# A routed two-layer kernel: its last three 128-row blocks go behind a branch on a count made on the chip

## The chip, the cores and the metric

One core of a Trainium2 chip runs the whole program. The metric is the device time of one execution in microseconds (us). Engines are named as in the profile: PE (TensorE matmuls), PEld (its weight loads), DVE (VectorE), ACT (ScalarE), POOL (GpSimd) and SP (SyncE, which issues DMAs here). A "q" behind an engine's name (POOLq, SPq) is its sequencer.

## What is computed

The input is x (8 x 3584 x 192). A softmax-weighted causal convolution of 7 taps per head group makes 28672 tokens of 192 values. Each token goes to the one of 8 experts whose embedding is nearest by cosine, and leaves it scaled by the gate weight:

```python
x = attn_out.reshape(B * S, D)                  # 28672 x 192
logits = xn @ en.T / tau
expert_idx = np.argmax(logits, axis=1)
for e in range(E):                              # 8 experts
    mask = expert_idx == e
    h = np.maximum(x[mask] @ w1[e], 0.0)        # 192 -> 1024
    out[mask] = gate_w[mask, None] * (h @ w2[e])  # 1024 -> 192
```

How many tokens an expert gets is known only when the program runs.

## The kernel before

**Routing.** The tokens come in 16 chunks of 1792. For each chunk, `mix` convolves, `route` and `rank` find the expert of every token and its place in that expert's list, and `scatter` (L626) writes the token's row (values in fp16 pairs, token number, gate weight) to `rows_d` in DRAM. Each expert has its own area there; behind the eight areas lies a dummy area. `pads` (L637) writes, behind each expert's list and into the dummy area, pad rows whose token number is N = 28672.

**Blocks.** The expert phase works on blocks of 1024, 512, 256 or 128 rows of one expert. The program's list of blocks, `self.subs`, is fixed when it is built; what each block holds is found on the chip by `select` (L656): from the counts so far it makes, per block, the offset of its expert's weights and its first row. `pick` (L836) calls it: as many blocks of n rows as are certain to exist, whatever the split over experts. Only in the last round, for n = 128, are the blocks rounded up: with `left` = 1792 rows not yet handed out, `pick(128, True)` makes (1792 + 8 x 127) // 128 = 21 blocks, which is enough for any split. In that call `select` counts the blocks that hold rows, expert by expert; `a` (L671) is their running sum, so its last element is their number. The blocks behind that number get the dummy area's address (L692 to L696).

**The last round.** `last_blocks` (L918) hands out 3 blocks of 1024 rows (each two sub-blocks of 512), 8 of 512, 8 of 256 and the 21 of 128, after all routing. It sorts them by keys so that the sizes alternate: the i-th of n in a class has the key (i + o) / (n + o), with o = 0.5 for the large and the middle class and 3 for the 128-row class. Written with A for a (sub-)block of 512 rows, M for 256 and s for 128, the order is

```
before: A A s A A A s s A s A s A s s A s A A A s s M s M s s M s M s A A s M s M s s M s M s
```

**One block** is `expert` (L772). A 128-row block takes its weights by two DVE copies into a slot: `copy_w1` (L717, copy at L729), which the preceding block issues at its end (L808), and `copy_w2` (L731). Then PE makes 40 matmuls into `h_ps` (L796); ACT writes relu (L800) and DVE the low half of the pair (L802), each in two instructions of 512 columns; DVE makes the gate factors `g` (L811); PE makes 24 matmuls into `o_ps` (L819); ACT scales (L824); POOL scatters 128 rows to the output by an indirect DMA (L826). Its `bounds_check=self.N - 1` with `oob_is_err=False` leaves out rows whose token number is N. A block of 512 has 40 wide matmuls and 96 of `o_ps`, one of 256 has 40 and 48. `fetch` (L736) loads a block's rows by two transposing DMAs and its token numbers by a third, from SP, up to three blocks ahead; there are three buffers `e_xT`.

**Order.** SP's queue stands in the order of the Python code. PE, DVE, ACT and POOL get theirs from the framework's scheduler, which lets the next block's `h_ps` matmuls fill PE's time between two parts of a block's `o_ps` matmuls. `run` (L930) drives all: its main loop (L985) ends when routing is done and all blocks are issued.

Of the kernel before, what the change touches and what calls it, by code (L numbers as in the profile page):

```python
# [15 lines left out]
I32 = mybir.dt.int32  # L16
# [10 lines left out]
E = 8  # L27
# [33 lines left out]
LEAD = 16.0  # L61
CAP = 6.0
MARGIN = 22
AHEAD_STEPS = 36


# [8 lines left out]
class _Moe:  # L75
# [580 lines left out]
    def select(self, n, k, last, name, cb):  # L656
        nc, cp = self.nc, self.cp
# [12 lines left out]
        a, ap, bs = one("a"), one("ap"), one("bs")  # L670
# [9 lines left out]
            out=ge[:, :, 1:], in0=a[:].unsqueeze(1).to_broadcast([1, k, E]),  # L680
# [4 lines left out]
            out=df, in0=df, in1=bs[:].unsqueeze(1).to_broadcast([1, k, E]),  # L685
# [3 lines left out]
        nc.vector.scalar_tensor_tensor(out=ro, in0=jf, scalar=float(n), in1=ro,  # L689
                                       op0=ALU.mult, op1=ALU.add)  # L690
        if last:
            nc.vector.tensor_scalar(out=tm, in0=jf, scalar1=-float(n),  # L692
                                    scalar2=float(self.dummy), op0=ALU.mult,
                                    op1=ALU.add)
            nc.vector.tensor_tensor(out=tm, in0=tm, in1=ge[:, :, E], op=ALU.mult)
            nc.vector.tensor_tensor(out=ro, in0=ro, in1=tm, op=ALU.add)  # L696
# [6 lines left out]
        if not last:  # L703
# [6 lines left out]
                out=self.start, in0=t, scalar=float(n), in1=self.start,  # L710
# [184 lines left out]
    def steer(self, spent):  # L895
# [9 lines left out]
        self.rate = min(self.rate, 3.0)  # L905
        self.pace = (NT * self.end - self.nput) / max(1.0, steps - MARGIN)
        if self.final:
            self.pace = 1.0
        early = 0
        for v in self.subs[self.at:]:  # L910
            if len(v) == 5 and v[4] > len(self.scatters):
                self.pace = max(self.pace, (v[4] - len(self.scatters))
                                / max(1.0, early - AHEAD_STEPS))
                break
# [3 lines left out]
    def last_blocks(self):  # L918
        self.now, self.final = self.cb[0:1, :], True
        self.need = len(self.scatters) + len(self.pend) + E + 1  # L920
        big = self.pick(1024)
        mid = self.pick(512) + self.pick(256)
        self.pads()
        small = self.pick(128, True)
        runs = [[((i + o) / (len(g) + o), b) for i, b in enumerate(g)]
                for g, o in ((big, 0.5), (mid, 0.5), (small, 3.0)) if g]
        for _, b in sorted(sum(runs, []), key=lambda v: v[0]):
            self.subs += b

    def run(self):  # L930
        self.left, self.rate = 0, 1.0
# [21 lines left out]
        done = dict.fromkeys(work, 0)  # L953
# [19 lines left out]
        a = self.dispatch()  # L973
# [8 lines left out]
            if i.engine in (self.nc.vector.engine, self.nc.scalar.engine):  # L982
                _dep(self.tc, i, end[i.engine].name, False)
        live, due, done, out = next(a, None), [0.0, 0.0], False, 0.0
        while live or self.pend or not done or self.at < len(self.subs):  # L985
            if self.at < len(self.subs):
                for v in self.expert():
                    self.steer(spent)
                    self.clock += STEP[v is OUT]
                    out = min(1.0, out + self.pace)  # L990
                    if out >= 1.0 and self.pend:
                        self.put(self.step)
                        out -= 1.0
                    due = [min(CAP, d + self.rate * t) for d, t in zip(due, v)]
                    while live and min(due) >= 0.0:
                        held = live is WAIT
                        if not held:
                            due = [d - t for d, t in zip(due, live)]
                            spent = [s + t for s, t in zip(spent, live)]
                        live = next(a, None)  # L1000
                        if held and live is WAIT:
                            break
            else:
                self.put()
                self.clock += 1.0
                if live:
                    live = next(a, None)
            if not live and not done:
                self.last_blocks()
                done = True  # L1010
        order.__exit__(None, None, None)


@with_exitstack
# [17 lines left out]
```

## Time and profile before

| | |
|---|---|
| time, median of 3 runs | 1249.96 us (1249.76, 1249.96, 1250.8) |
| the profiled execution: its own time | 1245.91 us |
| its span, first to last instruction | 1244.2 us |
| mean granted TensorE clock | 0.961 |
| PE busy | 1135.9 us (91%) |
| DVE, ACT, POOL busy | 61%, 48%, 44% |
| output scatters (L826) | 231 |
| matmuls of `o_ps` (L819) | 5544 |

The profiled execution took 4.05 us less than the median of the three runs. Engine rows of a timeline give the start in us from the span's start, the duration, the engine, the line, the operation, output and inputs, and how many instructions are merged; in brackets stands the idle time of the engine just before, and what ended it. Successive rows of PE overlap a little, as matmuls are pipelined; the differences between their starts don't. The page names in its third section the DMA queues: q0 carries the indirect DMAs of POOL, q8 and q14 carry instructions.

### The profile page before, as it was taken

To read this page: it belongs to the slowest core of one execution; us is meant where nothing else is said; L and a number is where in the kernel's file an instruction comes from. 1 tells how busy PE (TensorE), PEld (TensorE's weight loads), DVE (VectorE), ACT (ScalarE), POOL (GpSimd) and SP (SyncE) were. 2 spreads that over 40 slices of the span, in tenths; PEclk is the share of its full clock that TensorE was granted. 3 is DMA by queue.
4 is the path that set the end of the run, shared out by engine and by line. 5 is a ranking of instruction groups with operands and counts; after the bars stand their busy time and mean duration, and the time that the engine had idled before them with its cause. 6 is when DMAs were issued, how large, how long until landed. Compare 5 with 4: busy or idle time off the path is not lost.

```text
span 1244.2 us, 31794 instructions
## 1 busy us (share of the span) xinstructions
PE 1135.9 (91%) x10620; PEld 881.2 (71%) x10620; DVE 763.8 (61%) x2042; ACT 592.5 (48%) x1359; POOL 552.6 (44%) x525
## 2 busy tenths in 40 slices
PE   4765869899999899998999999989999999999998
PEld 2543758776677876766887667757877786898797
DVE  3899667885766856666766474653335544465364
ACT  4986335455564464563546463333333434333333
POOL 0074166573565554646745456672222121222222
PEclk9676889999999999999999999999999999999999
DMA  9745576566666596654657645333222131223121
GB/s 255 216 146 147 120 162 147 119 168 145 135 157 165 97 185 146 131 140 97 165 105 170 115 94 125 87 96 66 65 45 61 41 75 43 43 54 72 42 52 28
DMA packets 305962, 140.69 MB, mean 113 GB/s; under 512 B 247774, under 2 KB 296285, under 8 KB 305808
## 3 DMA queue, kind: packets, MB, share of 16 engines
q1 hardware_dynamic: 282000, 87.97, 34.1%
q0 software_dynamic: 23808, 50.69, 14.7%
q8 instruction: 94, 1.54, 0.5%
q14 instruction: 60, 0.49, 0.1%
HBM read 38.35 MB, written 51.35 MB: 72 GB/s over the span
## 4 chain that ended last, share of the span: by engine, by line
issue 27%; PE 15%; POOL 8%; DMA 2%; ACT 1%; DVE 1%; POOLq 1%; ACTq 0%; DVEq 0%
POOL out_dram L826 7%; PE h_ps L796 7%; PE o_ps L819 6%; PE conv_ps L388 1%; DMA rows_d<-rows,di 1%; POOL rows_d L627 1%; DMA out_dram<-y,e_mt 1%; DMA xtb<-rows 0%; POOLq L826 0%; ACT work L800 0%; ACT sq L401 0%; PE lg_ps L611 0%; ACT rows L437 0%; DVE work L802 0%; DVE rows L444 0%
## 5 line engine op out<-in xcount | busy, mean ns | idle before, releaser
L819 PE MATMUL o_ps<-work 128*128 128x192 f16 x5544 | 503.2, 248 | 21.1 <-DVE work L802 9.2
L819 PEld LDWEIGHTS <-work 128*128 128x128 f16 x5544 | 462.5, 98 | 60.4 <-DVE work L802 15.7
L826 POOL DMA_INDIRECT out_dram<-y,e_mt x231 | 257.0, 1113 | 479.1 <-ACT y L824 439.2
L802 DVE SCALAR_TENSOR_TENSOR work<-h_ps,work 128x512 f16<-128x512 f32 x462 | 314.4, 685 | 175.2 <-ACT work L800 169.7
L800 ACT ACTIVATE work<-h_ps 128x512 f16<-128x512 f32 x462 | 271.3, 596 | 240.3 <-PE h_ps L796 206.1
L627 POOL DMA_INDIRECT rows_d<-rows,di x256 | 281.2, 1098 | 140.7 <-issue 57.1
L796 PE MATMUL h_ps<-e_xT,res 128*128 128x512 f16 x1360 | 311.2, 380 | 8.5 <-DVE work L802 5.9
L796 PEld LDWEIGHTS <-res 128*128 x1360 | 131.5, 98 | 162.7 <-issue 20.2
L796 PE MATMUL h_ps<-e_xT,work 128*128 128x256 f16 (+1 forms) x2320 | 232.4, 256 | 14.8 <-DMA e_xT<-rows_d 10.6
L796 PEld LDWEIGHTS <-work 128*128 128x128 f16 x2320 | 193.6, 99 | 40.7 <-DMA e_xT<-rows_d 9.9
L824 ACT ACTIVATE y<-o_ps,g 128x192 f32<-128x192 f32 x231 | 94.2, 419 | 235.6 <-PE o_ps L819 213.7
L732 DVE COPY work<-res 128x3074 f16 x88 | 85.3, 969 | 163.9 <-PE o_ps L819 163.8
L388 PE MATMUL conv_ps<-xt,band 128*112 128x384 f32 x256 | 112.5, 542 | 13.6 <-ACT xt L391 5.2
L437 ACT CAST rows<-xt 112x768 f16<-112x768 f32 x64 | 53.0, 832 | 97.4 <-DMA rows_d<-rows,di 49.2
L391 ACT COPY xt<-conv_ps 112x384 f32<-112x384 f32 x128 | 60.4, 480 | 43.0 <-PE conv_ps L388 41.5
L401 ACT ACTIVATE sq<-xt 112x192 bf16<-112x192 f32 x204 | 73.6, 361 | 4.8
L444 DVE TENSOR_TENSOR rows<-xt,rows 112x512 f16<-112x512 f32 x64 | 43.9, 685 | 45.7 <-ACT rows L437 35.3
L388 PEld LDWEIGHTS conv_ps<-xt,band 128*112 128x112 f32 x256 | 42.8, 194 | 32.0 <-issue 13.1
L435 DVE TENSOR_TENSOR xt<-xt,x_p_s 112x768 f32<-112x768 f32 x64 | 58.5, 950 | 0.0
L729 DVE COPY work<-res 128x3072 f16 x58 | 55.5, 957 | 0.3 <-PE h_ps L796 0.3
L611 PEld LDWEIGHTS <-xtb 128*128 128x128 f16 x768 | 30.1, 98 | 26.1 <-DMA xtb<-rows 12.9
L611 PE MATMUL lg_ps<-ma,xtb 128*128 128x16 f16 x512 | 30.6, 171 | 14.0 <-ACT xtb L502 7.1
(157 smaller groups left out, 520.5 us busy)
## 6 DMA issues: line engine op xcount, KB each, us to landing
xt<-in_dram SPq DMA_DIRECT2D x8, 1536.0 KB
xt<-in_dram SPq DMA_DIRECT2D x7, 1440.0 KB
rows_d<-rows,di POOLq DMA_INDIRECT x256
out_dram<-y,e_mt POOLq DMA_INDIRECT x231
xtb<-rows SPq DMA_TRANSPOSE x224
res<-in_dram SPq DMA_DIRECT2D x4, 768.0 KB
work<-in_dram SPq DMA_DIRECT2D x4, 768.0 KB
e_xT<-rows_d SPq DMA_TRANSPOSE x184
```

What stands on the lines that cost most here:

```text
L388: self.behind(nc.tensor.matmul(out=ps, lhsT=self.band[:, h, :], rhs=xt[:, :, h * G:(h + 1) * G], start=True, stop=True))
L391: nc.scalar.copy(out=xc[:, :, h * G:(h + 1) * G], in_=ps)
L401: nc.scalar.activation(out=sq, in_=xc[:, t, :], func=AF.Square, accum_out=n2[:, t:t + 1])
L611: i = self.nc.tensor.matmul(out=lg[:, g * GX + a, :], lhsT=xT[:, u:u + 128], rhs=self.mb if k == 2 else self.ma, start=(k == 0), stop=(k = ...
L627: i = self.nc.gpsimd.indirect_dma_start(out=self.rows_d[:, :], out_offset=bass.IndirectOffsetOnAxis(ap=idx, axis=0), in_=src, in_offset=No ...
L732: self.nc.vector.tensor_copy(out=self.slot[:, S2:], in_=self.res[:, bass.ds(self.we + W2, RES - W2)])
L796: mm = nc.tensor.matmul(out=ps[:, c, :], lhsT=w1(o, b + c), rhs=xT[:, k, :], start=(i == 0), stop=(i == 4))
L800: self.step = nc.scalar.activation(out=hh[:, b:b + m, :], in_=ps, func=AF.Relu).ins
L802: nc.vector.scalar_tensor_tensor(out=hl[:, b:b + m, :], in0=ps, scalar=0.0, in1=hh[:, b:b + m, :], op0=ALU.max, op1=ALU.subtract)
L819: mm = nc.tensor.matmul(out=o, lhsT=h[:, c, q], rhs=w2[:, c, k:k + D], start=(c + i == 0), stop=(c == NFC - 1 and i == 2))
L824: self.step = nc.scalar.activation(out=y, in_=o, func=AF.Copy, scale=g[:, a:a + 1]).ins
L826: i = nc.gpsimd.indirect_dma_start(out=self.out[:, :], out_offset=bass.IndirectOffsetOnAxis(ap=mt[:, a, 0:1], axis=0), in_=y, in_offset=No ...
```

## The change

The 21 blocks of 128 rows are split: the last three (`TAIL`) are taken out of the sorted order and set at the end of `self.subs`. The main loop stops before them, their rows are still fetched in the main program, and their computation stands in a branch body. `select` copies its count of non-empty blocks to a new one-element tile, `real`. After the main loop every engine loads `real` into a register and compares: the body runs if the count is greater than `self.skip`, which is 21 - 3 = 18.

```diff
@@ select @@
         if last:
+            self.real = cp.tile([1, 1], I32, name="real")
+            nc.vector.tensor_copy(out=self.real, in_=a[:, E - 1:E])
@@ last_blocks @@
         small = self.pick(128, True)
+        self.skip = len(small) - TAIL
+        small, spare = small[:-TAIL], small[-TAIL:]
...
             self.subs += b
+        self.subs += sum(spare, [])
@@ run @@
-        while live or self.pend or not done or self.at < len(self.subs):
+        while live or self.pend or not done or self.at < len(self.subs) - TAIL:
...
+        while self.ready < len(self.subs):
+            self.fetch()
         order.__exit__(None, None, None)
+        real = self.nc.values_load(self.real[0:1, 0:1], min_val=0, max_val=len(self.subs))
+        with self.tc.If(real > self.skip):
+            while self.at < len(self.subs):
+                for _ in self.expert():
+                    pass
```

With 18 blocks in the sort, the keys of the 128-row class change, and with them the order of the last round (before the branch):

```
change: A A A A s A s A s A s A s s A A A s A s M s s M s M s M A A s M s s M s M s M s
```

The changed program's line numbers are 3 higher in `expert` and `fetch`, and 1 to 3 higher elsewhere.

On POOL, the end of the program before has the scatters of the routing's last rows (L627) and then 101 output scatters (L826) in a row:

```order
L627 DMA rows_d<-rows_91,di 230528x240 x3
L826 DMA out_dram<-y,e_mt 28672x192 x101
L1028 UNCONDITIONAL_BRANCH
L1028 ISA
```

In the change, the last three scatters stand behind the register load and the compare; the rows behind them, up to the last, are of the two ways through the branch and the program's end:

```order
L628 DMA rows_d<-rows_91,di 230528x240 x3
L829 DMA out_dram<-y,e_mt 28672x192 x98
L1020 TENSOR_LOAD real
L1021 COMPARE_AND_BRANCH
L829 DMA out_dram<-y,e_mt 28672x192 x3
L1021 UNCONDITIONAL_BRANCH
L1021 ISA
L1021 UNCONDITIONAL_BRANCH
L1041 ISA
```

The other engines have the same pair of rows ahead of their part of the three blocks.

On DVE, the end of the program before is the last 128-row block: its second weight copy, its gate factor, its two instructions on `h_ps`:

```order
L729 ISA
L729 COPY work<-res 128x3072
L802 SCALAR_TENSOR_TENSOR work<-h_ps,work 128x512
L732 ISA
L732 COPY work<-res 128x3074
L811 TENSOR_SCALAR g<-e_mt,work 128x1
L802 SCALAR_TENSOR_TENSOR work<-h_ps,work 128x512 x2
L1028 UNCONDITIONAL_BRANCH
```

In the change, the last block ahead of the branch has a block behind it in the list, and so the copy of that block's first weights (3072 columns) stands between its two instructions on `h_ps`:

```order
L735 COPY work<-res 128x3074
L814 TENSOR_SCALAR g<-e_mt,work 128x1
L805 SCALAR_TENSOR_TENSOR work<-h_ps,work 128x512
L732 ISA
L732 COPY work<-res 128x3072
L805 SCALAR_TENSOR_TENSOR work<-h_ps,work 128x512
L1020 TENSOR_LOAD real
L1021 COMPARE_AND_BRANCH
```

What moved is the second instruction on `h_ps`: it followed the first directly, and now it follows the copy.

On SP, `real` is not loaded at the end. The scheduler set the load among the DMAs of the last round, ahead of the transposes of its first block (a 512-row one):

```order
L745 TENSOR_LOAD sel_7936_12532
L745 ISA x2
L1020 TENSOR_LOAD real
L1020 ISA x2
L753 ISA
L753 DMA_TRANSPOSE e_xT<-rows_d 128x3x512
L753 ISA
L753 DMA_TRANSPOSE e_xT<-rows_d 128x1x512
```

Before, the same transposes stood directly behind the load of their own row number:

```order
L742 TENSOR_LOAD sel_7936_12532
L742 ISA x2
L750 ISA
L750 DMA_TRANSPOSE e_xT<-rows_d 128x3x512
L750 ISA
L750 DMA_TRANSPOSE e_xT<-rows_d 128x1x512
```

So on SP one register load with its two bookkeeping instructions came in, and every later DMA of SP is queued behind it.

## Rows read from the trace of the kernel before

**Rows 1.** The page: busy time, PE's slices of the span, and the granted clock.
```profile
PE 1135.9 (91%) x10620; PEld 881.2 (71%) x10620; DVE 763.8 (61%) x2042; ACT 592.5 (48%) x1359; POOL 552.6 (44%) x525
PE   4765869899999899998999999989999999999998
PEclk9676889999999999999999999999999999999999
```

**Rows 2.** Busy time of each engine by stretch: the last round.
```profile
core 0: us, PE busy (x) PEld busy (x) DVE busy (x) ACT busy (x) POOL busy (x), PEclk, DMA share, GB/s
846.30:1241.50 395.20, 389.84 (x3954) 316.65 (x3952) 192.20 (x297) 148.01 (x280) 99.84 (x94) 1.00 0.25 52
```

**Rows 3.** Timeline of PE: o_ps matmuls of 512-row blocks, and a 128-row block's start.
```profile
992.67 8.08 PE L819 MATMUL o_ps<-work 128*128 128x192 f16 x96
...
1018.46 8.08 PE L819 MATMUL o_ps<-work 128*128 128x192 f16 x96
1026.38 2.40 PE L796 MATMUL h_ps<-e_xT,work 128*128 128x128 f16 x40
1028.62 0.33 PE L819 MATMUL o_ps<-work 128*128 128x192 f16 x2
...
1039.23 8.08 PE L819 MATMUL o_ps<-work 128*128 128x192 f16 x96
...
1055.78 8.08 PE L819 MATMUL o_ps<-work 128*128 128x192 f16 x96
1063.70 8.80 PE L796 MATMUL h_ps<-e_xT,res 128*128 128x512 f16 x40
1072.34 8.08 PE L819 MATMUL o_ps<-work 128*128 128x192 f16 x96
```

**Rows 4.** Timeline of PE: o_ps matmuls of 256-row blocks near the end.
```profile
1187.46 3.46 PE L819 MATMUL o_ps<-work 128*128 128x192 f16 x40
...
1200.37 3.46 PE L819 MATMUL o_ps<-work 128*128 128x192 f16 x40
...
1217.99 3.46 PE L819 MATMUL o_ps<-work 128*128 128x192 f16 x40
```

**Rows 5.** DMA of q0 behind four output scatters (1211.2:1215, 1217.3:1220, 1230.3:1233, 1240.4:1244.2).
```profile
q0 software_dynamic: 48, 0.05, 3.8%
...
q0 software_dynamic: 48, 0.00, 1.0%
...
q0 software_dynamic: 48, 0.00, 1.1%
...
q0 software_dynamic: 48, 0.00, 0.7%
```

**Rows 6.** Timeline, all engines: around a weight copy near the end, and the last block.
```profile
1206.82 0.60 ACT L800 ACTIVATE work<-h_ps 128x512 f16<-128x512 f32 x1 [0.52 <-PE h_ps L796]
...
1206.94 0.95 DVE L729 COPY work<-res 128x3072 f16 x1
...
1207.81 0.68 DVE L802 SCALAR_TENSOR_TENSOR work<-h_ps,work 128x512 f16<-128x512 f32 x1
...
1237.35 0.60 ACT L800 ACTIVATE work<-h_ps 128x512 f16<-128x512 f32 x1 [0.52 <-PE h_ps L796]
...
1237.98 0.69 DVE L802 SCALAR_TENSOR_TENSOR work<-h_ps,work 128x512 f16<-128x512 f32 x1 [0.42 <-ACT work L800]
```

**Rows 7.** Timeline, all engines: from the last matmuls on.
```profile
1238.53 1.20 PE L819 MATMUL o_ps<-work 128*128 128x192 f16 x11
1238.73 0.77 PEld L819 LDWEIGHTS <-work 128*128 128x128 f16 x10 [0.18 <-DVE work L802]
1239.77 0.42 ACT L824 ACTIVATE y<-o_ps,g 128x192 f32<-128x192 f32 x1 [1.82 <-PE o_ps L819]
1240.46 0.98 POOL L826 DMA_INDIRECT out_dram<-y,e_mt  x1 [2.11 <-ACT y L824]
```

**Rows 8.** Line L1028 (the program's end): counts, duration ns min/median/max, first and last start.
```profile
L1028 POOLq DRAIN  x3: 40/113/3161, 1240.2 to 1243.9; - x3
L1028 SPq DRAIN  x3: 7/7/13, 1243.1 to 1243.7; - x3
```

**Rows 9.** Register loads of PE (L779) and of DVE (L725), the same columns.
```profile
L779 PEldq TENSOR_LOAD <-sel x30: 299/306/527, 272.4 to 837.7; - x30
L779 PEldq FUSED_REGOPS  x30: 146/151/165, 273.0 to 838.1; - x30
L725 DVEq TENSOR_LOAD <-sel x88: 300/308/596, 100.8 to 839.8; - x88
```

**Rows 10.** Instruction queue of the page, and of the stretch 1190:1245: packets, MB, share.
```profile
q8 instruction: 94, 1.54, 0.5%
...
q8 instruction: 5, 0.08, 0.6%
```

**Rows 11.** Timelines of DVE (812, 818) and SP (835): the last select and the last round's fetch.
```profile
812.37 0.32 DVE L679 TENSOR_TENSOR sl_ge<-sl_a,nums 1x168 f16<-1x168 f32 x1
...
818.51 0.15 DVE L702 CAST sel<-sl_ro 1x21 int32<-1x21 f32 x1
...
835.90 2.79 SPq L750 DMA_TRANSPOSE e_xT<-rows_d  x2
```

More of the change, by code (lines that the diff above doesn't have):

```diff
@@ L63 @@
 MARGIN = 22
+TAIL = 3
 AHEAD_STEPS = 36
```

## The prediction

> **What bounds the kernel now.** First the page: PE is busy for 91% of the span, and its slices stay at 8 or 9 tenths from the seventh on, where the granted clock reaches its top digit too [rows 1]. [...]
>
> Next, what a 128-row block costs. Since PE fills gaps of one block with matmuls of the next, no block has a beginning and an end of its own; I read it from the differences between the starts of the 96 `o_ps` matmuls of 512-row blocks [rows 3]. From 1055.78 to 1072.34 one block of 512 passes: 16.56 us. From 1018.46 to 1039.23 a 128 and a 512: 20.77, so the 128 costs 4.21 us. From 992.67 to 1018.46 two 128s and a 512: 25.79, so a second 128 in a row costs 5.02. It agrees with PE's own time: 40 matmuls from 1026.38 to 1028.62 are 2.24 us, and 24 of the 96 in the 7.92 us from 1018.46 to 1026.38 are 1.98, together 4.22 [rows 3]. Ahead of a 256, the second 128 costs 1217.99 - 1200.37 less 1200.37 - 1187.46, that is 17.62 - 12.91 = 4.71 [rows 4].
>
> **Are the three blocks empty?** If they are, the body is left out; if one of the 18 others were too few, it runs. The DMA queue of the output scatters tells it. The last four 128-row blocks of before each send 48 packets; the first of these four moves 0.05 MB, the other three 0.00 MB [rows 5]. A full block moves 128 x 768 bytes, 0.10 MB, and rows with the token number N are left out. So block 18 is about half full, and blocks 19 to 21 hold nothing but pads. The count is 18, the bar is 18, and 18 > 18 is false. The reference's inputs say the same: of the 1792 tokens that are left for the 128-row class, the eight experts have 176, 227, 89, 77, 160, 88, 146 and 829, which are 2+2+1+1+2+1+2+7 = 18 blocks, the last one with 61 rows (47 KB).
>
> **The change part by part**, against the profiled execution's 1245.91 us:
>
> 1. *Three 128-row blocks leave PE.* By the order of before, 16 of the 21 stand first after a larger block and 5 stand second in a row (2 ahead of a 512, 3 ahead of a 256). In the changed order 15 of the 18 stand first, 3 second (1 ahead of a 512, 2 ahead of a 256). What leaves is one first, one second ahead of a 512, one second ahead of a 256: 4.21 + 5.02 + 4.71 = **13.94 us**. Taken at the bare 4.21 each it would be 12.63, the lower bound of this term; nothing in the rows would make it more than 3 x 5.02 = 15.06. One seam is new, a 512 directly behind a 256; its matmuls stand like those of a 128 behind a 256, so I add nothing. The blocks' three scatters leave POOL too, which was idle for most of the stretch [rows 2].
>
> 2. *The weight copy for the first spare block.* It remains in the main program, between the last real block's two DVE instructions on `h_ps`. Near the end of before the same copy does this: ACT ends at 1207.42, the DVE instruction starts at 1207.81, 0.39 later, held by the copy. In the last block of before there is no copy, and it starts at 1237.98, 0.03 after ACT's end at 1237.95 [rows 6]. Elsewhere PE has the next block's matmuls to fill this; in the last block it hasn't, and it already waited 0.18 us for that DVE instruction [rows 7]. So the whole 0.39 - 0.03 = **+0.36 us** counts; bounds 0 (if covered) and 0.95 (the whole copy).
>
> 3. *The end: register load, compare, jump.* Each engine loads `real`, as PE and DVE load block numbers now: 0.31 us and 0.15 for bookkeeping behind it [rows 9], about 0.5. The compare and the jump aren't in the trace. What covers them: PE's last matmul ends at 1239.73, and SP passes its last wait at 1243.1, 3.4 us later [rows 7, 8]; in between come ACT, POOL's scatter (to 1241.44), and its landing. PE, DVE and ACT do their branch under this cover; SP meets its own long before. POOL alone is on the path, and there a drain that ends at 1240.2 + 3.16 = 1243.4 us [rows 8] covers what the sequencer does ahead of it, unless that lasts beyond 1.9 us after the scatter's issue. From below 0; from above, one fetch of code that nothing hides. An instruction packet alone takes 0.006 x 55 us x 16 engines / 5 = 1.06 us [rows 10], and the nearest row of a small DMA's whole way is the last scatter, from its issue at 1240.46 to SP's 1243.1: 2.6 us [rows 7, 8]. So a bare fetch is 1.06 to 2.6 us, and the most is 2.6 + 0.5 = 3.1; I take **+0.6**, near the lower end, as each engine but POOL has cover.
>
> 4. *The copy of the count, and SP's load of it.* One more cast on DVE, 0.15 us like its neighbour, in the chain of `select` after 812.7 [rows 11], where PE does wait for DVE; the register loads that the scheduler scattered among DVE's work there shift by a place or two. **+0.1**, bounds -0.5 and +0.5. On SP, the first fetch of the last round now stands behind the load of the count. The chain that makes the count is over by 818.66, and that fetch starts only at 835.90 [rows 11]: 17 us of cover, so nothing. The fetches of the three empty blocks stay, the last one behind the last real block's `h_ps`; they end under the cover of part 3.
>
> Sum: -13.94 + 0.36 + 0.6 + 0.1 = -12.9, so **1233.0 us** for an execution like the profiled one. The median of the three runs stands 4.05 above that execution; with the same difference, 1249.96 - 12.9, rounded, is **1237.0 us**, 1.0% less.
>
> **Rivals.**
>
> *A: the jump isn't covered.* PE's part of the three blocks is about 385 instructions, so the place PE jumps to lies 385 instructions ahead, and PE takes its code in packets of 1.54 MB / 94 = 16 KB [rows 10]. If PE's target isn't there, or POOL's, the engine stands until it is. With the 3.1 us of part 3 instead of 0.6, and the copy at its upper bound of 0.95, the sum is -13.94 + 0.95 + 3.1 + 0.1 = -9.8: **1240.2 us**. For it: packets arrive in order, one by one, so a jump over more than one meets code that nobody asked for. Against it: PE's cover of 3.4 us exceeds one such fetch, and POOL's jump is over a dozen instructions. [...]
>
> *B: the branch is taken.* It decides at a count of 19: then the three blocks run after the main program has emptied PE, the copy and the register load stand bare, and the three run in a row. Price: at least 2 x 5.02 + 4.22 = 14.3 us comes back, with 0.36 + 0.5 + 0.1 and up to some 2.6 us in which ACT, DVE and the pipelines start anew: -13.94 + 14.3 + 1.0 + 2.6 = +3.9 at most, **1253.9 us**, slower. For it: the count stands exactly at the bar, and one rounding or one off-by-one in it is enough. Against it: three scatters that moved no row [rows 5].
>
> *C: PE isn't what ends last.* If a queue behind PE (POOL's scatters, SP's fetches) set the pace, the time would stay: **1250 us**. Against it: 5.4 us of idle PE in 395 [rows 2].
>
> **How the numbers follow.** My forecast 0.80, A 0.14, B 0.04, C 0.02. Low end: the profiled execution's own sum, **1233.0**, which takes in both that runs differ by up to 4 us and the larger 15.06 of part 1. High end: A's 1240.2 plus 1.04 for the scatter of the runs (1249.76 to 1250.8), rounded up, **1241.5**. B and C, 0.06, lie outside. A measurement of this kernel can tell about 0.2%, 2.5 us, from no change. Both my forecast and A are faster by more: faster **0.94**, within 0.2% (C) **0.02**, slower (B) **0.04**.
>
> **What would show it.** In the changed profile: 228 output scatters and not 231; 5472 matmuls of `o_ps` (72 less) and 120 less into `h_ps`; the starts of 512-row blocks still 16.56 and 20.77 us apart, the granted clock still full in the last round. Part 2 shows as a wait of some 0.5 us of PE for DVE in the last block; part 3 as the time from the last matmul's end to the span's end, 4.5 us now (1239.73 to 1244.2). Over 7 us there, A is right. If scatters number 231, B is. If the starts of blocks in the last round move apart, the order matters and part 1 is wrong.

## The result and the profile after

The changed kernel takes 1238.2 us, the median of 6 runs (1234.27 to 1239.61); the kernel before, 6 runs (the three above among them), 1250.38 us (1249.76 to 1254.23). The medians differ by 12.2 us. The ratio of the runs is 0.9894, 95% interval 0.9872 to 0.9917: by the ratio 13.3 us less, by its interval 10.4 to 16.0. Forecast were 12.9. The profiled execution took 1238.18 us, with a span of 1236.5 us and a mean granted clock of 0.955 (before: 1244.2 and 0.961).

The page of the changed kernel, busy time and slices as in [rows 1], and two of its groups of instructions:

```profile
PE 1127.5 (91%) x10428; PEld 872.4 (71%) x10428; DVE 756.1 (61%) x2029; ACT 587.4 (48%) x1350; POOL 550.4 (45%) x522
PE   4675769899999899998989999999999999999998
PEclk9676879899999999999989999999999999999999
...
L822 PE MATMUL o_ps<-work 128*128 128x192 f16 x5472 | 497.8, 248 | 21.3 <-DVE work L805 9.9
L829 POOL DMA_INDIRECT out_dram<-y,e_mt x228 | 255.1, 1119 | 470.8 <-ACT y L827 434.0
```

There are 5472 matmuls of `o_ps` and 228 scatters. PE executes 192 matmuls fewer than in [rows 1]: 72 of `o_ps`, and so 120 into `h_ps`. Three blocks are out: the body of the branch is not run.

For a stage of its own I take the **last round** from the end of the last ACT instruction on `y` of the block ahead of it to the end of the program's last one: 846.54 + 0.43 = 846.97 to 1239.77 + 0.42 = 1240.19 before (the latter in [rows 7]), 851.79 + 0.42 = 852.21 to 1231.83 after. Busy time of each engine in that stretch, the kernel before:

```profile
core 0: us, PE busy (x) PEld busy (x) DVE busy (x) ACT busy (x) POOL busy (x), PEclk, DMA share, GB/s
846.97:1240.19 393.22, 389.17 (x3950) 316.33 (x3948) 191.73 (x297) 147.58 (x279) 98.86 (x93) 1.00 0.25 52
```

The same stretch of the changed kernel:

```profile
852.21:1231.83 379.62, 376.08 (x3758) 303.66 (x3756) 183.33 (x283) 142.56 (x270) 95.37 (x90) 1.00 0.25 54
```

The last round is 13.60 us shorter, and 13.09 of that is busy PE. But it begins 5.24 us later, in code that the two kernels share up to one DVE cast and the register loads around it; the eighth experiment and the last section come back to that.

The timeline of PE, three starts of 512-row blocks with one 128-row block between each two, as in [rows 3]:

```profile
930.60 8.08 PE L822 MATMUL o_ps<-work 128*128 128x192 f16 x96
...
951.37 8.08 PE L822 MATMUL o_ps<-work 128*128 128x192 f16 x96
...
972.13 8.08 PE L822 MATMUL o_ps<-work 128*128 128x192 f16 x96
```

They stand 20.77 and 20.76 us apart, as before: the price of a block did not move with its place.

The timeline of all engines at the end, where [rows 6, 7] showed the last block of before:

```profile
1228.64 0.60 ACT L803 ACTIVATE work<-h_ps 128x512 f16<-128x512 f32 x1 [0.52 <-PE h_ps L799]
...
1228.77 0.95 DVE L732 COPY work<-res 128x3072 f16 x1
...
1229.63 0.68 DVE L805 SCALAR_TENSOR_TENSOR work<-h_ps,work 128x512 f16<-128x512 f32 x1
1230.37 1.00 PE L822 MATMUL o_ps<-work 128*128 128x192 f16 x10 [0.30 <-DVEq L1021]
...
1231.41 0.42 ACT L827 ACTIVATE y<-o_ps,g 128x192 f32<-128x192 f32 x1 [2.17 <-PE o_ps L822]
1232.10 0.97 POOL L829 DMA_INDIRECT out_dram<-y,e_mt  x1 [2.26 <-ACT y L827]
```

ACT is done at 1229.24, DVE starts at 1229.63: 0.39 us later, held by the copy for a block that is never computed. PE stands 0.30 us until DVE's instruction ends at 1230.31 (the row names DVE's bookkeeping at the branch's line as the releaser).

Last, the lines of the branch (L1021) on the engines; columns as in [rows 8]:

```profile
L1021 DVEq COMPARE_BRANCH  x1: 72/72/72, 1229.7 to 1229.7; - x1
...
L1021 PEldq COMPARE_BRANCH  x1: 4017/4017/4017, 1231.0 to 1231.0; - x1
...
L1021 POOLq COMPARE_BRANCH  x1: 45/45/45, 1232.4 to 1232.4; - x1
...
L1021 POOLq INC_SWDGE_SEM  x1: 503/503/503, 1232.7 to 1232.7; - x1
```

and of the program's end (L1041), which answers to [rows 8]:

```profile
L1041 POOLq DRAIN  x3: 40/107/2296, 1233.2 to 1236.2; - x3
L1041 SPq DRAIN  x3: 7/7/13, 1235.6 to 1235.9; - x3
```

Two things stand here that the end of before did not have: PE spends 4.02 us in the jump, and POOL executes, on the way past the branch, an instruction of 0.50 us that the kernel doesn't write. From the last matmul's end to the span's end it is 1231.37 to 1236.49, **5.12 us**, where it was 4.48.

### The profile page after: what moved, and what is told of

Same layout as the page of the kernel before. It is cut to its first block, busy times and chain, and to the rows that moved or that the text cites. A ratio compares the mean times of both kernels' runs of the same rounds, so it can differ in the third digit from the quotient of the medians.

```text
span 1236.5 us, 31375 instructions
## 1 busy us (share of the span) xinstructions
PE 1127.5 (91%) x10428; PEld 872.4 (71%) x10428; DVE 756.1 (61%) x2029; ACT 587.4 (48%) x1350; POOL 550.4 (45%) x522
## 4 chain that ended last, share of the span: by engine, by line
PE 37%; issue 8%; POOL 3%; DMA 3%; ACT 1%; DVE 1%; POOLq 0%; ACTq 0%; DVEq 0%
PE h_ps L799 18%; PE o_ps L822 17%; POOL out_dram L829 2%; POOL rows_d L628 1%; PE conv_ps L389 1%; DMA rows_d<-rows,di 1%; DMA xtb<-rows 1%; DMA out_dram<-y,e_mt 1%; ACT work L803 1%; DVE work L805 0%; DMA rows_d<-xtb,padi 0%; ACT rows L438 0%; ACT sq L402 0%; PE lg_ps L612 0%; DVE work L735 0%
## 5 line engine op out<-in xcount | busy, mean ns | idle before, releaser
L822 PE MATMUL o_ps<-work 128*128 128x192 f16 x5472 | 497.8, 248 | 21.3 <-DVE work L805 9.9
L822 PEld LDWEIGHTS <-work 128*128 128x128 f16 x5472 | 458.5, 99 | 59.9 <-DVE work L805 15.9
L805 DVE SCALAR_TENSOR_TENSOR work<-h_ps,work 128x512 f16<-128x512 f32 x456 | 311.1, 687 | 169.0 <-ACT work L803 165.2
L803 ACT ACTIVATE work<-h_ps 128x512 f16<-128x512 f32 x456 | 267.5, 596 | 236.5 <-PE h_ps L799 205.5
L799 PE MATMUL h_ps<-e_xT,work 128*128 128x256 f16 (+1 forms) x2200 | 226.7, 259 | 15.2 <-DMA e_xT<-rows_d 10.2
L799 PEld LDWEIGHTS <-work 128*128 128x128 f16 x2200 | 187.4, 99 | 41.5 <-DMA e_xT<-rows_d 10.4
L735 DVE COPY work<-res 128x3074 f16 x85 | 82.3, 968 | 165.2 <-PE o_ps L822 161.2
```

What stands on the lines that cost most here:

```text
L735: self.nc.vector.tensor_copy(out=self.slot[:, S2:], in_=self.res[:, bass.ds(self.we + W2, RES - W2)])
L799: mm = nc.tensor.matmul(out=ps[:, c, :], lhsT=w1(o, b + c), rhs=xT[:, k, :], start=(i == 0), stop=(i == 4))
L803: self.step = nc.scalar.activation(out=hh[:, b:b + m, :], in_=ps, func=AF.Relu).ins
L805: nc.vector.scalar_tensor_tensor(out=hl[:, b:b + m, :], in0=ps, scalar=0.0, in1=hh[:, b:b + m, :], op0=ALU.max, op1=ALU.subtract)
L822: mm = nc.tensor.matmul(out=o, lhsT=h[:, c, q], rhs=w2[:, c, k:k + D], start=(c + i == 0), stop=(c == NFC - 1 and i == 2))
```

## The experiments

Stages as above; "end" is from the last matmul's end to the span's end. Both come from the trace of one execution. Kernels that compute the same blocks in the same order agree in the last round within 0.01 us (379.62, 379.62, 379.62 and 379.63, four executions).

| kernel | last round | end | PE's compare, ns | ratio to before (95%) |
|---|---|---|---|---|
| before | 393.22 | 4.48 | - | 1 |
| changed | 379.62 | 5.12 | 4017 | 0.9894 (0.9872 to 0.9917) |
| no_branch | 379.62 | 4.45 | - | 0.9901 (0.9864 to 0.9938) |
| order_only | 393.29 | 4.47 | - | 1.0006 (0.9986 to 1.0026) |
| taken | 393.62 | 4.49 | 80 | 1.0013 (0.9994 to 1.0032) |
| align | 379.62 | 5.21 | 396 | 0.9949 (0.9920 to 0.9978) |
| no_scatter | 379.63 | 4.65 | 3516 | 0.9914 (0.9893 to 0.9935) |
| tail2 | 384.62 | 4.40 | 399 | 0.9935 (0.9911 to 0.9960) |
| alternate | 377.47 | 5.09 | 3852 | 0.9864 (0.9842 to 0.9886) |

**1. no_branch.** The three blocks are left out for good: no count, no register load, no branch.

```diff
-            self.real = cp.tile([1, 1], I32, name="real")
-            nc.vector.tensor_copy(out=self.real, in_=a[:, E - 1:E])
...
-        real = self.nc.values_load(self.real[0:1, 0:1], min_val=0, max_val=len(self.subs))
-        with self.tc.If(real > self.skip):
-            while self.at < len(self.subs):
-                for _ in self.expert():
-                    pass
```

> The changed kernel without the copy of the count, its register loads, the compare and the body: the last three 128-row blocks are fetched and the first one's weight copy is made, as in the change, but nothing computes them on any path. Theory (what leaves is the PE time of three blocks; the jump is covered by ACT, the last scatter and its landing): the last round stays as in the change, 379.6 us from the last o_ps result of the last block ahead of it (852.21) to its own last result (1231.83), within 0.3; from PE's last matmul to the span's end 4.9 to 5.2 us, against 5.12 in the change and 4.48 before, since the 0.64 us more are the landing of a last scatter that now moves real rows. Rival (PE's jump of 4.02 us, or POOL's load and jump, is on the path): PE's last matmul to the end falls to 4.5 us or less, and the time is 0.6 us or more below the change's 1238.2.

Its median is 1237.1 us (4 runs, 1234.47 to 1241.55). The last round is that of the changed kernel to 0.01 us: having the branch costs nothing up to the last matmul. The end is 0.66 us shorter. Its program's end (L1034):

```profile
L1034 POOLq DRAIN  x3: 40/113/3139, 1232.7 to 1236.4; - x3
L1034 SPq DRAIN  x3: 7/7/13, 1235.8 to 1236.1; - x3
```

Its last matmul ends at 1232.22; POOL's drain ends at 1232.72 + 3.14, 3.64 us later. In the changed kernel that is 1233.25 + 2.30 - 1231.37, 4.17 us. So something that POOL or SP waits for came half a microsecond later, and that is most of the 0.66. The expectation, 4.9 to 5.2, missed, and its rival's 4.5 or less came true: something of the branch is on the path. The expectation had put the longer end down to a last scatter that moves real rows. By the trace's semaphore events that scatter has landed 2.93 us after the last matmul here, and the empty one of before at 2.83: 0.10 us.

**2. order_only.** The order of the change, and all 21 blocks computed in it; as in no_branch, the count, its loads and the branch are left out too.

```diff
-        while live or self.pend or not done or self.at < len(self.subs) - TAIL:
+        while live or self.pend or not done or self.at < len(self.subs):
```

> The changed kernel's order of blocks with the three empty blocks computed at the end in the main program, no branch. Theory (the gain is the three blocks' PE time, the order gives about 1 us of it by having fewer second 128s in a row, which comes back here as three more in a row): the last round takes 379.6 - 0.36 + 4.2 + 2 x 4.7 to 3 x 5.0, 393 to 395 us, against 393.2 before; time 1250 to 1252, the same as before. Rival (the order itself brings a good part of the gain): 390 us or less in the last round, time 1247 or less.

The last round's busy time:

```profile
849.40:1242.69 393.29, 389.04 (x3950) 316.50 (x3948) 192.08 (x297) 147.45 (x280) 99.12 (x93) 1.00 0.25 52
```

The order alone is worth 0.07 us, and in the time nothing that can be measured. All of the gain is the three blocks: at the end of the list they take 393.29 - 379.62 = 13.67 us.

**3. taken.** The bar is one lower, so that the count of 18 runs the body. ("Taken" means here that the body runs; the jump is what skips it.)

```diff
-        self.skip = len(small) - TAIL
+        self.skip = len(small) - TAIL - 1
```

> The changed kernel with the bar lowered by one, so that the same count takes the branch and the three empty blocks are computed in the body. Theory: as order_only, plus what it costs that the body can't fill the gaps of the last block ahead of it: register loads of about 0.5 us and a restart of PE, ACT and DVE, 1 to 4 us; no stall of PE at the compare, as the body follows it in the program: compare 0.1 us. Time 1252 to 1255, 0.1 to 0.4% over before. Rival (a branch costs by itself some us on every engine, taken or not): PE's compare takes 4 us here too and the time is 1256 or more.

The last round is 393.62 us, 0.40 more than before, and the end 4.49. The last four evictions, from the timeline of ACT:

```profile
1237.13 0.42 ACT L827 ACTIVATE y<-o_ps,g 128x192 f32<-128x192 f32 x1 [2.17 <-PE o_ps L822]
1242.59 0.42 ACT L827 ACTIVATE y<-o_ps,g 128x192 f32<-128x192 f32 x1 [2.58 <-PE o_ps L822]
1247.93 0.42 ACT L827 ACTIVATE y<-o_ps,g 128x192 f32<-128x192 f32 x1 [0.73 <-DVE work L805]
1251.13 0.42 ACT L827 ACTIVATE y<-o_ps,g 128x192 f32<-128x192 f32 x1 [1.99 <-PE o_ps L822]
```

The last block ahead of the branch ends at 1237.55, 379.62 us into the last round, and three blocks of 5.46, 5.34 and 3.20 us follow: 14.00 in all, against 13.67 in order_only. PE falls through the compare in 0.08 us. So a body that is run behind a branch costs 0.33 us over the same order without it.

**4. align.** 53 small transposes at the start (two PE instructions each), into a tile that nothing reads, shift the place of PE's compare within its instruction packets.

```diff
+        fill = self.ps("r", [128, 4, E], F16, "fill_ps")
+        for _ in range(53):
+            nc.tensor.transpose(out=fill[:, 0, :], in_=hi[:, 0:128], identity=self.idh[:E, :E])
```

> The changed kernel with 53 more small transposes (106 PE instructions) at the very start, where PE waits some 5 us for the convolution's bands; their result isn't used. In the change PE met the compare about 235 to 240 instructions after it asked for its last packet of 16 KB, and asked for the target's packet 1.2 us after the compare began. [...] Rival (any jump that isn't to the next instruction costs PE its 4 us): 4 us again. If the stall was on the path after all, the end shortens by 0.3 us or more.

The line of the branch, PE's row:

```profile
L1025 PEldq COMPARE_BRANCH  x1: 396/396/396, 1238.2 to 1238.2; - x1
```

The jump falls from 4.02 to 0.40 us, and the end stays at 5.21. So the stall on PE depends on where the jump stands in its code, and that PE stands still costs this kernel nothing. In the trace of before the 94 packets of 16 KB start one by one, one for 255 PE instructions on average (23736 rows of PE, PEld and their sequencer between the starts of the first and the last). In the changed kernel the last of them ahead of the compare starts some 240 instructions before it, by a count of the trace's rows, and the next packet only at 1232.19, 1.17 us after the compare began at 1231.02; it is the only one that starts while PE stands there, and so I take it to hold the jump's target. Here, by the same count, it is some 70 instructions. With the 384 matmuls and weight loads of the three blocks jumped over, the target lay some 620 instructions behind that packet's start in the changed kernel and some 450 here: 4.02 us and 0.40. How much code is at hand at a jump no run shows. The time of this kernel as a whole is another matter: 1244.88 us, higher than the changed kernel's, and all of that ahead of the last round (it begins at 859.49).

**5. no_scatter.** The branch's body keeps everything but its scatters.

```diff
+            if self.body:
+                continue
             i = nc.gpsimd.indirect_dma_start(
...
+        self.body = True
         with self.tc.If(real > self.skip):
```

> The changed kernel with the three output scatters left out of the branch body (the body computes the three blocks and writes none of their rows). In the change POOL carries out, on the way that skips the body, an instruction INC_SWDGE_SEM of 0.50 us that makes up for the semaphores of the three skipped scatters; two DMA landings at 3.31 and 3.47 us after PE's last matmul follow the last scatter's at 2.93, and SP's last waits go on only then. Without any branch those two are missing and the end is 4.45 us instead of 5.12. Theory (these 0.66 us are that instruction's late landings alone): without scatters in the body POOL has nothing to make up, no landing comes after 2.95, and the end takes 4.4 to 4.6 us, with PE's compare still at 4 us. Rival (they are the register loads and jumps): 5.0 to 5.2 us again. The last round stays at 379.6.

The row of PE's compare (L1024) and that of the program's end (L1044):

```profile
L1024 PEldq COMPARE_BRANCH  x1: 3516/3516/3516, 1228.9 to 1228.9; - x1
...
L1044 POOLq DRAIN  x3: 40/113/2471, 1230.5 to 1233.6; - x3
```

With no scatter to skip, the instruction of 0.50 us is gone from POOL. The drain ends at 1230.48 + 2.47, 3.70 us after the last matmul (1229.26), not 4.17, and the end falls from 5.12 to 4.65, to within 0.19 us of no_branch. That looks as if `INC_SWDGE_SEM` were worth 0.47 us. The trace of the changed kernel says otherwise: the instruction raises the semaphores of the three skipped scatters once each, and these events come 1.79 to 1.81 us after the last matmul, 1.7 us before SP goes on. What SP waits for is the last real scatter. SP's waits at the end, the changed kernel and then this one (us in total, times, longest):

```profile
SPq L1041 <- DMA out_dram<-y,e_mt: 3.0, 1, 3.0
...
SPq L1044 <- DMA out_dram<-y,e_mt: 2.5, 1, 2.5
```

That scatter raises its semaphore in 16 steps. In the changed kernel 15 of them are there at 2.93 us and the last at 3.46; SP goes on at 3.48. Here the last is there at 2.99. (The two events at 3.31 and 3.47 that the expectation took for the instruction's are the sixteenth of a load of SP, L757, and this sixteenth of the scatter.) Beside it stands the instruction packet that starts while PE is in its compare: it is under way from 0.82 to 2.29 us in the changed kernel and from 0.81 to 1.81 here, 1.47 and 1.00 us, a difference of the same 0.47. That load of SP, the last one of token numbers, has a late part beside the packet too. It has 144 packets; in the changed kernel 135 of them have started by 1.42 us, and the other 9, a sixteenth, start at 2.27 to 2.33, as the instruction packet ends. Queue q1 from 1232.3 to 1232.85 us, and from 1233.62 to 1233.75:

```profile
q1 hardware_dynamic: 135, 0.00, 13.0%
...
q1 hardware_dynamic: 9, 0.00, 8.4%
```

The traces side by side, in us after the last matmul:

| kernel | instruction packet | a sixteenth of the load starts | last scatter's last event | end |
|---|---|---|---|---|
| before | none | - | 2.83 | 4.48 |
| no_branch | none | - | 2.93 | 4.45 |
| tail2 | 0.64 to 1.58 | - | 2.82 | 4.40 |
| no_scatter | 0.81 to 1.81 | 1.79 | 2.99 | 4.65 |
| alternate | 0.69 to 2.16 | 2.16 | 3.44 | 5.09 |
| changed | 0.82 to 2.29 | 2.27 | 3.46 | 5.12 |
| align | 1.40 to 2.35 | 2.33 | 3.56 | 5.21 |

The end follows the scatter's last event by 1.52 to 1.66 us in each, with `INC_SWDGE_SEM` and without it. In the last four rows that event follows the packet's end by 1.17 to 1.28 us. That the packet holds back one of the scatter's 16 parts, by 0.53 us in the changed kernel, is my reading of these rows and not shown: they are one execution each, and no run moves the packet alone. Why the packet took 1.47 us in one execution and 1.00 in another is open; packets of this size take 0.88 to 2.37 us in these traces, and in align it took 0.95 with `INC_SWDGE_SEM` beside it.

**6. tail2.** Two blocks in the branch in place of three, and so one of the empty ones computed.

```diff
-TAIL = 3
+TAIL = 2
```

> The changed kernel with TAIL = 2: two blocks behind the branch, one empty block still computed in the sorted order. Theory (each block is worth its PE time, more where it stands second in a row): by the intervals of before and of the change the last round takes 384.2 us (379.6 plus 4.6), within 0.4, and the time is some 4.6 us over the change, 1242 to 1244, with a spread of runs of several us that comes from ahead of the last round. PE's jump is 260 instructions from a place 128 later in the program, so the target lies in the packet behind the one it is in, and its compare takes 0.05 to 0.5 us instead of 4.02; the end stays at 5.0 to 5.2. Rival (the gain of the change comes with the last of the three, or with the branch as such): within 1 us of the change in the last round. Rival on the jump (any far jump stalls): 4 us.

The last round is 384.62 us: the third block is worth 5.00. The end is 4.40, where I had expected 5.0 to 5.2. The line of the branch (L1021):

```profile
L1021 POOLq INC_SWDGE_SEM  x1: 503/503/503, 1231.2 to 1231.2; - x1
...
L1021 PEldq COMPARE_BRANCH  x1: 399/399/399, 1233.9 to 1233.9; - x1
```

The scheduler set the main program's last two scatters behind the branch on POOL, so the instruction ran at 1231.2, 3.2 us ahead of the last matmul's end at 1234.39. The instruction packet was early too: it ended 1.58 us after the last matmul, and 1.2 us more, as in the other kernels, is still ahead of the 2.82 at which the last scatter lands. Either of the two would give the short end, so this run doesn't tell them apart. PE's jump is short here too (0.40 us): the last packet ahead of the compare starts some 100 instructions before it, and the jump is shorter by a block's 128, so the target lay some 360 behind that start.

**7. alternate.** A version against both kernels: no 128-row block stands second in a row in the main program, and the weight copy for the first spare block waits until the branch is decided.

```diff
-        self.counts, self.pace = {}, 1.0
+        self.counts, self.pace, self.hold = {}, 1.0, -1
...
-        if self.copied > at or at == len(self.subs):
+        if self.copied > at or at in (len(self.subs), self.hold):
...
-        runs = [[((i + o) / (len(g) + o), b) for i, b in enumerate(g)]
-                for g, o in ((big, 0.5), (mid, 0.5), (small, 3.0)) if g]
-        for _, b in sorted(sum(runs, []), key=lambda v: v[0]):
+        runs = [[((i + 0.5) / (len(g) + 0.5), b) for i, b in enumerate(g)]
+                for g in (big, mid) if g]
+        for j, (_, b) in enumerate(sorted(sum(runs, []), key=lambda v: v[0])):
             self.subs += b
+            if j and small:
+                self.subs += small.pop(0)
+        self.subs += sum(small, [])
         self.subs += sum(spare, [])
+        self.hold = len(self.subs) - TAIL
@@ run @@
+        self.hold = -1
         with self.tc.If(real > self.skip):
```

> The changed kernel with two edits: the weight copy for the first block of the body is made in the body, and the 18 blocks of 128 rows are set one by one between the larger blocks, so that none stands second in a row. Theory: a second 128 in a row costs 0.8 us more than a first ahead of a 512 and 0.5 us more ahead of a 256, and the change has one and two of them, 1.8 us; the copy costs 0.35 us in the last block (its interval 4.83 against 4.48). The last round falls from 379.6 to 377.3 to 377.8 us, the last interval to 4.4 to 4.5. Time 2.1 us below the change, about 1236, less than the spread of single runs. Rival (the stalls only move to other places, as PE's gaps depend on what stands next): 379 us or more.

Its median is 1234.14 us (4 runs, 1230.34 to 1234.62) beside 1250.14 of before (13 runs). The last round is 377.47 us, 2.15 less than the changed kernel's. Its last block, from the timeline of all engines:

```profile
1224.91 2.12 PE L822 MATMUL o_ps<-work 128*128 128x192 f16 x22 [0.19 <-DVE work L805]
1225.28 0.69 DVE L805 SCALAR_TENSOR_TENSOR work<-h_ps,work 128x512 f16<-128x512 f32 x1 [0.43 <-ACT work L803]
...
1227.06 0.42 ACT L827 ACTIVATE y<-o_ps,g 128x192 f32<-128x192 f32 x1 [1.82 <-PE o_ps L822]
```

DVE now waits for ACT, not for a copy, PE goes through 22 matmuls without the gap of 0.30, and the last interval between evictions is 4.49 us, where it was 4.83. So 0.34 of the 2.15 us is the copy, and 1.81 is left for the order: as much as three second blocks become first ones by the prices of [rows 3, 4], (5.02 - 4.21) + 2 x (4.71 - 4.21) = 1.81. The end, 5.09, still has the instruction packet beside it (0.69 to 2.16 us). This version beats the kernel before; against the changed kernel the last round says 2.15 us, but the two ratios' intervals overlap, and the two were not run side by side.

**8. pad_before and pad_tile.** Why is align slow? The 53 transposes alone, put into the kernel before with the edit of align (pad_before); then the same into one more group of columns of a tile that is there anyway (pad_tile):

```diff
-        ps = self.ps("l", [128, 4, E], F16, "em_ps")
+        ps = self.ps("l", [128, 5, E], F16, "em_ps")
...
+        for _ in range(53):
+            nc.tensor.transpose(out=ps[:, 4, :], in_=hi[:, 0:128], identity=self.idh[:E, :E])
```

> The kernel before, with the 53 small transposes of the run align at its start and nothing else. The run align was 6.7 us slower than the change at the median, and its profile shows the loss ahead of the last round (859.49 against 852.21 at its start), with stretches at the lower clock that the change doesn't have. If the transposes do that whatever the rest of the program, this run's median lies 4 to 9 us over before's, and its last round still takes 393.2 us. If align's loss came from the change together with the transposes, or by chance, it lies within 2.5 us of before.

> The kernel before with the same 53 small transposes, now into unused columns of the tile em_ps that the embeddings' transposes already use; in the run pad_before they took a PSUM buffer of their own from the ring that the convolutions use, which shifts that ring's two buffers by one for the rest of the program. pad_before was 8.35 us slower than before, all of it ahead of the last round. If the ring's shift did that, this run lies within 2.5 us of before. If it was the transposes themselves (0.5 us later embeddings, PE work at the start, code moved by 106 instructions), it is 5 us or more slower again. The last round takes 393.2 us either way.

pad_before is slower than before by 8.35 us (1258.49 to 1250.14; ratio 1.0055, 1.0033 to 1.0076), pad_tile by 6.96 (1255.62 to 1248.66, 9 runs of before; 1.0057, 1.0036 to 1.0077). The last round of both is 393.22 us, exactly that of before: all of it lies ahead. That a new tile shifts the ring of PSUM buffers is ruled out as the cause by pad_tile. What the cause is stays open.

## Why the prediction was right, and where not

**What bounds the kernel: right.** PE in the last round, at a granted clock of 1.00 before and after: busy 389.17 of 393.22 us and 376.08 of 379.62. 13.09 of the 13.60 us that the stage lost is PE's busy time.

**Part 1 and part 2: right, to 0.02 us.** Together they were to give -13.94 + 0.36 = -13.58, and the last round gave -13.60. The copy by itself: the last interval between evictions went from 4.48 to 4.83 us, +0.35, and with the copy held back it is 4.49. Of the two terms, the new seam was costed at nothing, and that holds: between the same neighbours, the evictions of a 128, a 256, a 128 and a 512 take 7.33 + 5.64 + 7.63 + 12.96 = 33.56 us before, and without the second 128 7.27 + 6.28 + 15.74 = 29.29 after: 4.27 for the block that left, against the 4.21 of a first one. That the whole agrees to 0.02 us when this seam alone is 0.06 off is in part luck. The blocks are empty, as [rows 5] had it.

**Part 3: the right size for a wrong reason.** Forecast +0.6, measured +0.64. The step put it on the register load, the compare and the jump, of POOL above all. None of them is on the path there: POOL's register load begins 0.50 us after the last matmul, the last scatter 0.73, as in no_branch; its compare takes 45 ns, and the drain behind it absorbs that and `INC_SWDGE_SEM`, for which the text had no term. What came later is the landing of the last scatter, which the step had counted as cover and given no price: 3.46 us after the last matmul where it was 2.83. Of these 0.63 us, 0.10 stands in no_branch too (2.93), where the last scatter also has real rows; 0.53 lies between its fifteenth event and its sixteenth, which came 1.17 us behind the instruction packet's end. The bounds, 0 to 3.1, held that; that the size agrees is luck.

Of PE the step said that its jump is covered, and PE's standing is, though its own bounds for a fetch were too low: 1.06 to 2.6 us, measured 4.02. It began 0.35 us ahead of the last matmul's end and ended 3.67 after it; SP passes its last wait at 4.17. The cover sufficed by 0.5 us, half a microsecond that the late landing itself had added. In no_branch SP passes that wait at 3.48. With the landing there, a jump that ends at 3.67 would thus have been on the edge (in no_scatter it took 3.52 us and ended at 3.2).

**Part 4: not separable.** +0.1 was the forecast; the start of the last round differs between executions by far more (846.97 before, 852.21 after, and 853.06 in no_branch, which lacks part 4).

**The sum: right in the median, not in the profiled execution.** The two stages give -13.60 + 0.64 = -12.96 against -12.9. The forecast for "an execution like the profiled one", 1233.0 us, missed the profiled 1238.18 by 5.2, which is the 5.24 us by which the last round began later. The step that took the difference of 4.05 us between the profiled execution and the median into account is what held: 1237.0 against 1238.2. Where in the spread of its runs a profiled execution falls is chance: 4.05 us under the median before, at the median after.

**The rivals.** A named what the changed kernel shows, a packet that starts only 1.17 us after PE's compare began and a jump of 4.02 us, and even the right engine; the cover decided against it: 5.12 us at the end, not over 7. What A had not named are transfers that come late beside that packet: a sixteenth of SP's load, which starts at 2.27 us as the packet ends (2.29), and the last event of the scatter, 0.53 us behind the fifteenth. B did not occur, and its price of +3.9 us was mis-sized: taken measured +0.40 in the last round and nothing at the end. The error is mainly the 2.6 us in which ACT, DVE and the pipelines were to start anew, an estimate of the author that no run shows. The timeline of PE in taken, from the last matmuls ahead of the branch to the first ones in its body:

```profile
1236.09 1.00 PE L822 MATMUL o_ps<-work 128*128 128x192 f16 x10 [0.30 <-DVE work L805]
1236.93 2.40 PE L799 MATMUL h_ps<-e_xT,work 128*128 128x128 f16 x40
```

The body's matmuls follow without a gap: PE falls through its compare and waits for no other engine there. With that, a wrong guess of the count would have cost nothing that can be measured. C did not occur either, as part 1 shows.

## What to carry to other kernels

In a stage that one engine fills, price a block by the distance between equal instructions with and without it, seam by seam (4.21, 4.71 and 5.02 us here), and sum those; here the total came out to 0.02 us. The branch at this program's end was not free (an end of 5.12 us against 4.45 in no_branch) although every engine's own share of it was covered: look for an instruction packet that starts during the jump, and for the output transfer that is under way beside it. Where the packet ended early (tail2) or there was none, the last scatter landed at 2.8 to 2.9 us; where it ended later, at up to 3.56. Prepare nothing for a body that will mostly be skipped ahead of the branch if the preparation stands in the last block's chain (0.34 us here).

## What the runs showed of the hardware

**The skipped scatters' semaphores.** `INC_SWDGE_SEM` took 0.503 us on POOL each time. In the changed kernel it raised three semaphores and in tail2 two, one for each scatter that was skipped; they are the ones that the last scatters of before raise. No end hung on it: its events came 1.7 us before SP went on (changed kernel, align, alternate: 1.79 to 1.81 us after the last matmul).

**SP went on behind the last of the scatter's 16 events.** In the changed kernel 15 of 16 were there at 2.93 us and SP went on at 3.48, behind the sixteenth at 3.46. In the four executions of the table that have both an instruction packet and a late sixteenth of a load, the sixteenth started within 0.02 us of the packet's end.

**The price of a jump.** On PE 4.02, 3.85 and 3.52 us in the changed kernel, alternate and no_scatter, 0.40 in align and in tail2, 0.08 where it falls through (taken); on POOL, ACT, SP and DVE 45 to 72 ns in the changed kernel. The instruction queue in the DMA view of the changed kernel, from 1231.0 to 1236.5 us (packets, MB, share):

```profile
q8 instruction: 2, 0.03, 2.7%
```

The first is the one taken for the target's. It begins 1.17 us after the compare, takes 1.47, and PE goes on 1.38 later: 4.02 in all, of which the transfer itself is little more than a third.

**Executions differ by the granted clock ahead of the last round.** The same code, in three stretches of the kernel before:

```profile
170.00:240.00 70.00, 55.48 (x555) 47.62 (x555) 47.43 (x128) 30.73 (x73) 46.56 (x40) 0.90 0.66 149
...
560.00:640.00 80.00, 72.03 (x702) 58.80 (x701) 55.41 (x180) 35.99 (x85) 48.09 (x43) 0.98 0.51 118
...
760.00:845.00 85.00, 79.04 (x692) 56.48 (x691) 43.78 (x149) 29.26 (x56) 56.50 (x59) 1.00 0.38 101
```

and of the changed kernel:

```profile
170.00:240.00 70.00, 55.30 (x542) 46.54 (x539) 47.59 (x126) 29.96 (x71) 45.17 (x40) 0.85 0.67 153
...
560.00:640.00 80.00, 70.64 (x697) 57.64 (x695) 54.27 (x181) 35.11 (x84) 50.92 (x43) 0.96 0.52 117
...
760.00:845.00 85.00, 80.35 (x654) 54.02 (x652) 47.13 (x155) 30.79 (x58) 58.73 (x61) 0.98 0.38 102
```

The granted clock (third column from the end) is lower in each, by 0.05, 0.02 and 0.02. An estimate from these rows, length times difference, is 3.5 + 1.6 + 1.7 = 6.8 us, of the size of the 5.24 us; other stretches go the other way (0.79 and 0.80 up to 170 us). Over the 47 runs of before that stood beside the experiments, a lower mean granted clock goes with a longer time (correlation -0.56, some 6 us for 0.01). That the clock is the cause of the delay is likely by that, not shown: the rows don't tell which of the two follows the other, nor what made the clock fall in one execution and not in the other.

**106 tiny PE instructions cost 6.7 to 8.4 us.** They stand in the first ten microseconds, keep PE busy for some 1.1 us (pad_before: 1.68 us in that stretch, before 0.54) and lengthen the program by more than themselves, ahead of the last round, in three kernels (pad_before 8.35, pad_tile 6.96, align 6.7 beside the changed kernel). Open.
